# Attention and MLP mixer on one core: batches in pairs on 128 partitions, attention in 64x64 array tiles, TensorE order by hand

## The chip, the cores and the metric

One core of one Trainium2 chip. The metric is the device time of one execution in microseconds (us). The engines are TensorE (PE, with its weight loads shown apart as PEld), VectorE (DVE), ScalarE (ACT), GpSimd (POOL) and SyncE (SP, which only issues DMA here). No second core runs, so a run is called fast when it lies within 1.5% of the fastest of the same kernel. Medians are over all runs of a kernel.

## The reference, cut to what matters

```python
# attention: 8 batches, 12 heads, 448 positions, 64 wide
scores = matmul(q, k^T) / 8 - log(448)
x = matmul(1 / (1 + exp(-scores)), v)          # heads side by side: x is [8, 448, 768]

# mixer: token sizes 448 -> 256 -> 448, channel sizes 768 -> 1536 -> 768
h = relu(x^T @ w_tok1) @ w_tok2
u = x + h^T
out = u + relu(u @ w_ch1) @ w_ch2              # float32
```

## The kernel before

Both kernels load or cast to 16 bits and accumulate in 32-bit PSUM. The sequence of 448 is split as position = 4p + j with p on 112 partitions. One batch is one unit of work: its attention is woven with the mixer of the batch before it, and a scheduler decides TensorE's final order.

```python
J = 4; P = S // J                      # 112 partitions
# loads: POOL queue, 32 to 16 bit in flight, runs of 64 floats (256 bytes)
nc.gpsimd.dma_start(out=t_ap, in_=src[b].rearrange("h (p j) e -> p j h e", j=J))

# scores of ONE head: hi picks 64 of 128 rows of the array; the next matmul uses the same rows
for half, ps in ((0, ta), (1, tb)):
    for ci in range(2):
        nc.tensor.matmul(out=ps[:, ci, 0:S],
            lhsT=qkTt[64*hi : 64*hi+64, 1, 2*half+ci, :],
            rhs=qkTt[64*hi : 64*hi+64, 0, :, :], ...)
    # ... sigmoid by ACT, 112 x 896 at a time

# attention times V: the two heads of a pair fill the two column halves
for hi in (1, 0):
    for c in (3, 2, 1, 0):
        nc.tensor.matmul(out=xat[64*hi : 64*hi+64, :], lhsT=vf[:, c, h, :], rhs=at[:, c, :], ...)

# second token product, made twice: transposed (input of the channel stage) and natural
def ytrans(db, ps):   # 2 matmuls of 448 columns, then uT = xT + ps by DVE
def ynat(j, half, ps):  # 2 matmuls of 384 columns, then u_nat = x_nat + ps by DVE
# ch1: 12 x 6 matmuls of 448 columns; ch2: 8 x 12 of 384 columns, 112 rows of output each

for b in range(B):
    ac = attention_chunks(b + 1) if b + 1 < B else []
    weave(ac, mixer_chunks(b))
```

Of the kernel before, what the change touches and what calls it, by code (L numbers as in the profile page):

```python
# [19 lines left out]
def kernel(  # L20
# [10 lines left out]
):  # L31
    nc = tc.nc
# [5 lines left out]
    J = 4  # L38
    P = S // J
    NPAIR = H // 2  # L40
    NDB = D // 128
    NCB = CC // 128
    DH = D // 2
    att_scale = 1.0 / math.sqrt(E)
# [9 lines left out]
    make_identity(nc, ident)  # L54
    bias_t = pc.tile([128, 1], FP32, name="att_bias")
    nc.vector.memset(bias_t[:, :], att_bias)

    par = {"qk": 0, "m": 0}

    w_tok1_t = pc.tile([P, J, TT], FP16, name="w_tok1_t")  # L60
# [5 lines left out]
    qkv_tiles = {}  # L66
    xmem = {}

    def emit_qkv_dma(b):
        qf = pa.tile([P, J, H, E], FP16, tag="qkv", bufs=6, name=f"q_f16_{b}")  # L70
        kf = pa.tile([P, J, H, E], FP16, tag="qkv", bufs=6, name=f"k_f16_{b}")
        vf = pa.tile([P, J, H, E], FP16, tag="qkv", bufs=6, name=f"v_f16_{b}")
        for t_ap, src in ((qf, q), (kf, k), (vf, v)):
            nc.gpsimd.dma_start(  # L74
                out=t_ap[:, :, :, :],
                in_=src[b].rearrange("h (p j) e -> p j h e", j=J),
            )
        qkv_tiles[b] = (qf, kf, vf)

    def emit_weight_dma():  # L80
        nc.gpsimd.dma_start(
            out=w_tok1_t[:, :, :], in_=moe_w_tok1.rearrange("(p j) t -> p j t", j=J)
        )
        nc.gpsimd.dma_start(
            out=w_tok2_s[:, :, :], in_=moe_w_tok2.rearrange("(tc t) s -> t tc s", tc=2)
        )
        nc.gpsimd.dma_start(
            out=w_ch1_t[:, :, :], in_=moe_w_ch1.rearrange("(db d) c -> d db c", db=NDB)
        )
        nc.gpsimd.dma_start(  # L90
            out=w_ch2_t[:, :, :], in_=moe_w_ch2.rearrange("(cb c) d -> c cb d", cb=NCB)
        )
        nc.vector.tensor_copy(
            out=w_tok2_n[:, :, :, :],
            in_=w_tok2_s.rearrange("t c (p j) -> t c j p", j=J),
        )

    def attention_chunks(b):
        qf, kf, vf = qkv_tiles[b]
        qkT = {}  # L100
        attnT = {}
        xT = pa.tile([128, NPAIR, S], FP16, tag="xT", bufs=2, name=f"xT_{b}")
        x_nat = pa.tile([P, J, D], FP16, tag="x_nat", bufs=2, name=f"x_nat_{b}")
        xmem[b] = (xT, x_nat)

        def t_full(pair):
            def f():
                tqt = pp.tile([128, 2, J, P], FP16, tag="t", bufs=1, name=f"tq_{b}_{pair}")
                for qk0, src in ((1, kf), (0, qf)):
                    for j in range(J):  # L110
                        nc.tensor.transpose(  # L111
                            out=tqt[:, qk0, j, :],
                            in_=src[:, j, 2 * pair : 2 * pair + 2, :],
                            identity=ident[:P, :P],
                        )
                qkTt = pa.tile(
                    [128, 2, J, P], FP16, tag="qkT", bufs=3, name=f"qkT_{b}_{pair}"
                )
                nc.vector.tensor_copy(out=qkTt[:, :, :, :], in_=tqt[:, :, :, :])  # L119
                qkT[pair] = qkTt  # L120

            return f

        def qk_group(i, hi):
            def f():
                at = pa.tile(
                    [P, J, S], FP16, tag="attnT", bufs=3, name=f"attnT_{b}_{i}_{hi}"
                )
                attnT[(i, hi)] = at
                pq = par["qk"]  # L130
                ta = pp.tile([P, 2, 512], FP32, tag=f"qk{pq}", bufs=1, name=f"qkA_{b}_{i}_{hi}")
                tb = pp.tile([P, 2, 512], FP32, tag=f"qk{1 - pq}", bufs=1, name=f"qkB_{b}_{i}_{hi}")
                par["qk"] ^= 1
                qkTt = qkT[i]
                for half, ps in ((0, ta), (1, tb)):
                    for ci in range(2):
                        nc.tensor.matmul(  # L137
                            out=ps[:, ci, 0:S],
                            lhsT=qkTt[64 * hi : 64 * hi + 64, 1, 2 * half + ci, :],
                            rhs=qkTt[64 * hi : 64 * hi + 64, 0, :, :],  # L140
                            start=True,
                            stop=True,
                        )
                    nc.scalar.activation(  # L144
                        out=at[:, 2 * half : 2 * half + 2, :],
                        in_=ps[:, :, 0:S],
                        func=SIGMOID,
                        bias=bias_t[:P, :],
                        scale=att_scale,
                    )  # L150

            return f

        def av_chunk(pair):
            def f():
                xat = pp.tile([128, S], FP32, tag="xa", bufs=1, name=f"xa_{b}_{pair}")
                for hi in (1, 0):
                    at = attnT[(pair, hi)]
                    h = 2 * pair + hi
                    for c in (3, 2, 1, 0):  # L160
                        nc.tensor.matmul(  # L161
                            out=xat[64 * hi : 64 * hi + 64, :],
                            lhsT=vf[:, c, h, :],
                            rhs=at[:, c, :],
                            start=(c == 3),
                            stop=(c == 0),
                        )
                nc.scalar.activation(out=xT[:, pair, :], in_=xat[:, :], func=COPYF)

            return f  # L170

        def bt_double(pair):
            def f():
                xb = pp.tile(
                    [P, J, 2, 128], FP16, tag="t", bufs=1, name=f"xb_{b}_{pair}"
                )
                for pi in (1, 0):
                    for j in range(J):
                        nc.tensor.transpose(  # L179
                            out=xb[:, j, pi, :],  # L180
                            in_=xT[:, pair + pi, 112 * j : 112 * j + 112],
                            identity=ident[:, :],
                        )
                nc.vector.tensor_copy(  # L184
                    out=x_nat[:, :, 128 * pair : 128 * pair + 256], in_=xb[:, :, :, :]
                )

            return f

        chunks = [t_full(0), t_full(1)]  # L190
        for i in range(NPAIR):
            chunks.append(qk_group(i, 0))
            if i + 2 < NPAIR:
                chunks.append(t_full(i + 2))
            if i >= 1:
                chunks.append(av_chunk(i - 1))
            chunks.append(qk_group(i, 1))
            if i == 3 or i == 5:
                chunks.append(bt_double(i - 3))
        chunks.append(av_chunk(NPAIR - 1))  # L200
        chunks.append(bt_double(NPAIR - 2))
        return chunks

    def mixer_chunks(b):
        xT, x_nat = xmem[b]
        chunks = []

        h1T = pa.tile([128, 2, D], FP16, tag="h1T", bufs=2, name=f"h1T_{b}")
        uT = pa.tile([128, NDB, S], FP16, tag="uT", bufs=1, name=f"uT_{b}")
        u_nat = pa.tile([P, J, D], FP32, tag="u_nat", bufs=1, name=f"u_nat_{b}")  # L210
        h2aT = pa.tile([128, NCB, S], FP16, tag="h2aT", bufs=1, name=f"h2aT_{b}")
        outs = pa.tile([P, J, D], FP32, tag="outs", bufs=1, name=f"outs_{b}")

        def tok1(half, tcb, ps):
            for j in range(J):
                nc.tensor.matmul(  # L216
                    out=ps[:, :],
                    lhsT=w_tok1_t[:, j, 128 * tcb : 128 * tcb + 128],
                    rhs=x_nat[:, j, DH * half : DH * half + DH],
                    start=(j == 0),  # L220
                    stop=(j == J - 1),
                )
            nc.scalar.activation(
                out=h1T[:, tcb, DH * half : DH * half + DH], in_=ps[:, :], func=RELU
            )

        def ytrans(db, ps):
            for tcb in (1, 0):
                nc.tensor.matmul(
                    out=ps[:, :],  # L230
                    lhsT=h1T[:, tcb, 128 * db : 128 * db + 128],
                    rhs=w_tok2_n[:, tcb, :, :],
                    start=(tcb == 1),
                    stop=(tcb == 0),
                )
# [97 lines left out]
    for c in attention_chunks(0):  # L333
        c()
# [35 lines left out]
```

## Time and profile before

| quantity | before |
|---|---|
| median, 4 runs | 543.12 us (541.00 to 544.24) |
| span of the profiled run | 541.1 us |
| TensorE busy | 94% |
| first matmul | 15.3 us |
| attention of batch 0 without a mixer | up to about 67 us, counted back from the later batches |
| then seven woven batches | 60.18 us each |
| last mixer and store | the remaining 52.4 us |

From the page of the kernel before come three lines: busy time by engine (share of the span, number of instructions), TensorE's busy tenths in 40 equal slices, and the shares of the chain of work that ended last.

```profile
PE 508.4 (94%) x3040; PEld 284.0 (52%) x3040; DVE 201.1 (37%) x346; ACT 225.8 (42%) x273; POOL 58.7 (11%) x34
...
PE   0789899999999999999999999999999999998994
...
PE 92%; DVE 3%; DMA 2%; ACT 1%; issue 1%; POOL 0%; POOLq 0%; DVEq 0%; ACTq 0%
```

TensorE binds: the chain runs through it for 92% of the span. The next view is the busy time by engine in chosen stretches of the same kernel (stretch, its length, busy us and instructions of each engine, granted clock, DMA share, GB/s).

```profile
30.00:90.00 60.00, 56.72 (x246) 24.07 (x245) 14.86 (x26) 34.68 (x41) 9.09 (x4) 1.00 1.94 116
210.00:270.00 60.00, 59.87 (x381) 34.18 (x379) 24.93 (x43) 27.99 (x34) 6.84 (x3) 1.00 0.63 58
```

In the woven stretch the first pair of numbers says that TensorE stood still for 0.13 of 60 us. Busy is not the same as well used, though. The timeline shows it (start, length, engine, line, operation, out<-in, partitions x elements, count). Lengths overlap, because matmuls are pipelined; the useful number is the distance from one start to the next.

```profile
22.70 0.95 PE L137 MATMUL qkA_0_1_138<-qkT_0_104 64*112 64x448 f16 x2
...
199.28 0.38 PE L161 MATMUL xa_0_1631<-attnT_0_1_1578,v_f_3_927 112*64 112x448 f16 x1
199.30 0.38 PE L161 MATMUL xa_0_1631<-attnT_0_0_1550,v_f_3_927 112*64 112x448 f16 x1
199.50 0.35 PE L161 MATMUL xa_0_1631<-attnT_0_1_1578,v_f_3_927 112*64 112x448 f16 x1
199.51 0.35 PE L161 MATMUL xa_0_1631<-attnT_0_0_1550,v_f_3_927 112*64 112x448 f16 x1
...
200.17 0.58 PE L137 MATMUL qkA_1_1_1642<-qkT_1_1536 64*112 64x448 f16 x2
200.59 0.54 PE L137 MATMUL qkB_1_1_1643<-qkT_1_1536 64*112 64x448 f16 x2
201.06 0.37 PE L242 MATMUL yn1a_1650<-h1T_1499,w_tok_n 128*112 128x384 f16 x1
```

Two value matmuls (L161), one per column half, start 0.02 us apart and the next two 0.2 us later: two share the time of one. The scores (L137) use 64 of 128 rows and get no such company: four of them take 0.89 us, from 200.17 to 201.06, so 0.22 each. At 22.70 the same pair of scores is listed with 0.95 us instead of 0.58: TensorE ran at half clock during the first stage. The trace's own clock record agrees: its first entry is full clock from 72.23 us on. The window view prints a granted clock of 1.00 before that only because the record has no entry there.

### The profile page before, as it was taken

Reading aid. Unit: us, or ns where it says so; the run is one execution under the profiler, and the core shown is the slowest. Engines: PE = TensorE matmul, PEld = TensorE weight load, DVE = VectorE, ACT = ScalarE, POOL = GpSimd, SP = SyncE. Lnnn points to the kernel's source line nnn. Section 1 sums busy time; section 2 is a strip of 40 time slices with the busy share of each in tenths; the row PEclk is TensorE's granted clock in tenths of the full one; section 3 lists DMA queues with packets and bytes.
Section 4 is the critical chain, followed back from the end, with each engine's and each line's share of the span. In section 5 each row is a group of like instructions: output and inputs, shape, how many; then the busy total and the mean of one; then the engine's idle time right before and its main releaser. Section 6 shows DMA issues by size and latency. Waiting matters only on the chain.

```text
span 541.1 us, 6968 instructions
## 1 busy us (share of the span) xinstructions
PE 508.4 (94%) x3040; PEld 284.0 (52%) x3040; DVE 201.1 (37%) x346; ACT 225.8 (42%) x273; POOL 58.7 (11%) x34
## 2 busy tenths in 40 slices
PE   0789899999999999999999999999999999998994
PEld 0433354576456654565456654565456644574463
DVE  0200054424542265324542264324542363325431
ACT  0356455424734274525634274435633274331000
POOL 8303300201030001101030102001000000000000
PEclk9999999999999999999999999999999999999998
DMA  9999980906497090909195190909000200002002
GB/s 98 185 212 164 132 52 2 102 2 126 28 60 43 28 127 1 102 1 143 12 76 28 60 95 6 97 1 154 1 1 0 98 7 1 1 1 102 1 1 102
DMA packets 133198, 33.14 MB, mean 61 GB/s; under 512 B 129600, under 2 KB 131392, under 8 KB 132272
## 3 DMA queue, kind: packets, MB, share of 16 engines
q0 software_dynamic: 132144, 21.69, 62.6%
q1 hardware_dynamic: 1024, 11.01, 6.1%
q8 instruction: 23, 0.38, 0.3%
q14 instruction: 7, 0.06, 0.0%
HBM read 43.38 MB, written 11.01 MB: 101 GB/s over the span
## 4 chain that ended last, share of the span: by engine, by line
PE 92%; DVE 3%; DMA 2%; ACT 1%; issue 1%; POOL 0%; POOLq 0%; DVEq 0%; ACTq 0%
DMA k_f_0_77<-in_k_dram 2%; DVE h2aT_4318 L265 1%; PE xa_4_310 L161 0%; PE xa_0_166 L161 0%; PE xa_3_282 L161 0%; PE xa_2_244 L161 0%; PE xa_1_205 L161 0%; POOL q_f_0_76 L74 0%; DVE u_nat_4317 L249 0%; PE c_0a_4496 L271 0%; PE c_0a_4144 L271 0%; PE c_0a_3584 L271 0%; PE c_1a_3055 L271 0%; PE c_0a_3018 L271 0%; PE c_2a_2527 L271 0%
## 5 line engine op out<-in xcount | busy, mean ns | idle before, releaser
L258 PEld LDWEIGHTS <-w_ch_t 128*128 128x128 f16 x576 | 53.3, 98 | 57.5 <-issue 13.4
L242 PEld LDWEIGHTS <-w_tok_n 128*112 128x112 f16 x128 | 13.7, 128 | 14.3 <-issue 13.3
L216 PEld LDWEIGHTS <-w_tok_t 112*128 112x128 f16 x128 | 11.6, 102 | 10.1 <-issue 5.7
L111 PE MATMUL tq_0_95<-ident,k_f_0_77 112*128 112x112 f16 x4 | 0.6, 294 | 15.3 <-DMA k_f_0_77<-in_k_dram 15.3
L271 PEld LDWEIGHTS <-h2aT_4318 128*112 128x112 f16 x96 | 12.4, 130 | 4.4 <-DVE h2aT_4318 L265 1.3
L271 PEld LDWEIGHTS <-h2aT_936 128*112 128x112 f16 x96 | 12.2, 130 | 3.9 <-issue 1.0
L271 PEld LDWEIGHTS <-h2aT_2068 128*112 128x112 f16 x96 | 12.2, 130 | 3.9 <-issue 1.0
L271 PEld LDWEIGHTS <-h2aT_2634 128*112 128x112 f16 x96 | 12.2, 130 | 3.9 <-issue 1.0
L271 PEld LDWEIGHTS <-h2aT_370 128*112 128x112 f16 x96 | 12.2, 130 | 3.9 <-issue 1.0
L271 PEld LDWEIGHTS <-h2aT_1502 128*112 128x112 f16 x96 | 12.2, 130 | 3.9 <-issue 1.0
L271 PEld LDWEIGHTS <-h2aT_3760 128*112 128x112 f16 x96 | 12.2, 130 | 3.9 <-issue 1.0
L271 PEld LDWEIGHTS <-h2aT_3200 128*112 128x112 f16 x96 | 12.2, 130 | 3.9 <-issue 1.0
L111 PEld LDWEIGHTS <-k_f_0_77 112*128 112x128 f16 x24 | 2.2, 130 | 20.4 <-DMA k_f_0_77<-in_k_dram 15.3
L161 PEld LDWEIGHTS <-v_f_0_78 112*64 112x64 f16 x48 | 4.2, 150 | 9.6 <-issue 9.6
L144 ACT ACTIVATE attnT_0_0_117<-qkA_0_0_118,att_bias 112x896 f16<-112x896 f32 x1 | 1.0, 1007 | 16.6 <-PE qkA_0_0_118 L137 16.6
L119 DVE COPY qkT_0_104<-tq_0_95 128x896 f16<-128x896 f16 x1 | 0.6, 625 | 15.4 <-PE tq_0_95 L111 15.4
L74 POOL DMA_DIRECT2D v_f_7_3191<-in_v_dram x1 | 2.3, 2279 | 30.1 <-PE xa_5_3168 L161 30.1
L74 POOL DMA_DIRECT2D v_f_3_927<-in_v_dram x1 | 2.3, 2277 | 30.1 <-PE xa_5_904 L161 30.1
L74 POOL DMA_DIRECT2D v_f_4_1493<-in_v_dram x1 | 2.3, 2277 | 30.1 <-PE xa_5_1470 L161 30.1
L74 POOL DMA_DIRECT2D v_f_5_2059<-in_v_dram x1 | 2.3, 2277 | 30.1 <-PE xa_5_2036 L161 30.1
L74 POOL DMA_DIRECT2D v_f_6_2625<-in_v_dram x1 | 2.3, 2277 | 30.1 <-PE xa_5_2602 L161 30.1
L184 DVE COPY x_nat_94<-xb_4_349 112x1024 f16<-112x1024 f16 x1 | 0.7, 691 | 11.8 <-PE xb_4_349 L179 11.8
(1442 smaller groups left out, 1233.5 us busy)
## 6 DMA issues: line engine op xcount, KB each, us to landing
w_ch_t<-in_moe_w_ch_dram POOLq DMA_DIRECT2D x2, 2304.0 KB, 26.8
out_dram<-outs_371 SPq DMA_DIRECT2D x1, 1344.0 KB, 6.4
out_dram<-outs_937 SPq DMA_DIRECT2D x1, 1344.0 KB, 6.4
out_dram<-outs_1503 SPq DMA_DIRECT2D x1, 1344.0 KB, 6.3
out_dram<-outs_2069 SPq DMA_DIRECT2D x1, 1344.0 KB, 6.4
out_dram<-outs_2635 SPq DMA_DIRECT2D x1, 1344.0 KB, 6.4
out_dram<-outs_3201 SPq DMA_DIRECT2D x1, 1344.0 KB, 6.2
out_dram<-outs_3761 SPq DMA_DIRECT2D x1, 1344.0 KB, 6.2
```

The source lines that it names most:

```text
L74: nc.gpsimd.dma_start(out=t_ap[:, :, :, :], in_=src[b].rearrange("h (p j) e -> p j h e", j=J),)
L111: nc.tensor.transpose(out=tqt[:, qk0, j, :], in_=src[:, j, 2 * pair : 2 * pair + 2, :], identity=ident[:P, :P],)
L119: nc.vector.tensor_copy(out=qkTt[:, :, :, :], in_=tqt[:, :, :, :])
L144: nc.scalar.activation(out=at[:, 2 * half : 2 * half + 2, :], in_=ps[:, :, 0:S], func=SIGMOID, bias=bias_t[:P, :], scale=att_scale,)
L161: nc.tensor.matmul(out=xat[64 * hi : 64 * hi + 64, :], lhsT=vf[:, c, h, :], rhs=at[:, c, :], start=(c == 3), stop=(c == 0),)
L184: nc.vector.tensor_copy(out=x_nat[:, :, 128 * pair : 128 * pair + 256], in_=xb[:, :, :, :])
L216: nc.tensor.matmul(out=ps[:, :], lhsT=w_tok1_t[:, j, 128 * tcb : 128 * tcb + 128], rhs=x_nat[:, j, DH * half : DH * half + DH], start=(j = ...
L242: nc.tensor.matmul(out=ps[:, :], lhsT=w_tok2_n[:, tcb, j, :], rhs=h1T[:, tcb, DH * half : DH * half + DH], start=(tcb == 1), stop=(tcb == 0),)
L258: nc.tensor.matmul(out=ps[:, :], lhsT=w_ch1_t[:, db, 128 * cb : 128 * cb + 128], rhs=uT[:, db, :], start=(db == NDB - 1), stop=(db == 0),)
L265: nc.vector.tensor_scalar(out=h2aT[:, cb, :], in0=ps[:, :], scalar1=0.0, scalar2=None, op0=MAX)
L271: nc.tensor.matmul(out=ps[:, :], lhsT=h2aT[:, cb, 112 * j : 112 * j + 112], rhs=w_ch2_t[:, cb, DH * half : DH * half + DH], start=(cb == N ...
```

## The change

The intent is to fill the array. Two batches share the partitions (64 positions of each, sequence = 7p + j), so the mixer works on all 128 rows. In attention a matmul is 64x64, and four of them (two heads by two batches, each in another quarter of the array) follow each other. The channel stage gets its input by transposing the finished natural sum rather than by a second token product. Loads go in pieces of one head pair and in runs of 1792 bytes, K before Q (before, Q came first). Q and K go over SP, and POOL casts them (DVE the very first pair); V is cast in flight. TensorE's order is fixed by hand.

```diff
-    J = 4
+    J = 7
     P = S // J
+            for b in range(2):      # load: 64 partitions per batch, one head pair
+                eng.dma_start(
+                    out=t[64 * b : 64 * b + 64, :, :, :],
+                    in_=src[2 * g + b, 2 * i : 2 * i + 2].rearrange("h (p j) e -> p h j e", j=J),
+                )
 # ... cut: for Q and K eng is SP and a POOL copy casts to 16 bits; for V it is POOL, cast in flight
+        def scores(i, j):
+            for b in range(2):
+                for h in range(2):
+                    nc.tensor.matmul(
+                        out=ps[64 * b : 64 * b + 64, h, 0:S],
+                        lhsT=kT[i][64 * h : 64 * h + 64, j, b, :],
+                        rhs=qT[i][64 * h : 64 * h + 64, b, :, :], ...)
 # ... cut: one sigmoid of 128 x 896
+        def values(i):
+            for j in range(J):
+                for h in range(2):
+                    for b in range(2):
+                        nc.tensor.matmul(
+                            out=ps[b][64 * h : 64 * h + 64, :],
+                            lhsT=vf[64 * b : 64 * b + 64, h, j, :],
+                            rhs=attn[(i, j)][64 * b : 64 * b + 64, h, :], ...)
 # ... cut: copies to xT by ACT; back(i): seven transposes into the natural layout
-        def ytrans(db, ps):
+        def tok2(j):       # natural sum u by DVE, then a 16-bit copy u16 of it by DVE
+        def uturn(j):      # six transposes of u16, copied to uT by ACT
 # ... cut: ch1 in pieces of 512 and 384 columns, ch2 14 x 12 matmuls of 384 columns
+    with tc.manual_schedule(engines={mybir.EngineType.PE}):
+        for _, _, f in attention_atoms(0):
+            f()
+        for g in range(NG):
+            front, rest = mixer_atoms(g)     # front: first token product
 # ... cut: rest is woven with attention_atoms(g + 1) by weights in us
```

Below, a group is a pair of batches, and the first stage is the attention of group 0, which runs without a mixer.

## The prediction

> **What bounds it now.** TensorE. The busy table gives it 94% of 541 us, the chain of waits 92%; ACT has 42%, DVE 37%, POOL 11%. Three stages (timeline): the first matmul starts at 15.3 us, waiting for K by DMA. Batch 0's attention runs alone to about 67 us, with 448-column matmuls 0.37 us apart; from about 72 us on the pitch is 0.19. The Trainium skill, "TensorE: Matmul & The Clock Gate", Part 1, has these two states (half clock until the array is kept busy); the PEclk row does not show it. From 90 to 450 us the windows show TensorE busy 59.87 of each 60 us, 381 matmuls: 60 us per batch, 120 per pair. The last mixer takes 490 to 533, then some 7 us of eviction and store.
>
> **Warm pitches (timeline).** 448 columns 0.190, 384 columns 0.163, 128-column transpose 0.056, 64-row scores 0.21. Two 64-column value matmuls already start 0.01-0.02 us apart, 0.19 per pair: column tiles overlap. A change of tile shape costs some 0.1 us (eight value matmuls: 0.89 instead of 0.76). Before, pitches sum to about 55 of 60 us; the rest is switches and unpaired value matmuls.
>
> **After, TensorE per pair of batches** (estimate from these pitches): ch1 72x0.217+72x0.163=27.4; ch2 168x0.163=27.3 (fewer than 192, all 128 rows full instead of 112); transposes 168x0.056=9.4; tok1 and tok2 each 28 concurrent pairs, 4.6; scores and values each 42 quads of 0.19 if all four tiles overlap, 8.0; sum 89. The transposed token product (24 matmuls of 448, 4.6 us per pair of batches) goes; 42 transposes, 2.4 us, come. Shape switches about 60x0.1=6, small waits 3-5: about 99 us a pair instead of 120. The skill, "TensorEngine Tiling (Array Packing)", Key Properties, says that tiles run independently and that a mode switch drains; the trace shows the overlap for two tiles, none for four.
>
> **Other engines per pair:** ACT 42x0.91 for sigmoids (batch-0 spacing) plus 12x0.5, 8x0.45, 7x0.7: about 53; DVE about 41; POOL 12 casts and 12 V issues. None binds except locally: the token stage needs about 1.8 us of DVE per j against 1.0 of TensorE.
>
> **Stages.** Smaller, contiguous 1792-byte loads on SP: first matmul at about 8 us. Attention of pair 0 alone: ACT 44 us, TensorE at half clock about 50-56, in-order waits: ends near 70. Three woven groups of 99: 367. Last mixer without attention: 4.6+12+55=72: 439. Evictions and store now go by 128x768 pieces: +3.
>
> **Predicted: 442 us, range 416 to 472.** Nearly all of the gain lies on the critical path, since TensorE bounds. Chances: faster 0.97, within 2% 0.015, slower 0.015.
>
> **Shown right by:** four score matmuls starting within about 0.05 us, some 0.2 us per quad; windows of about 99 us per group with TensorE above 93% busy; pair 0's half-clock pitch to about 70 us; DMA packets far fewer, first matmul near 8 us.
>
> **Wrong if:** four tiles overlap only in twos (0.38 per quad: +16 us per group, about 495 in all); weight loads of 64 columns serialise the quads (0.25: +5 per group); the fixed order leaves TensorE waiting for PSUM banks, the token stage's DVE or POOL casts; w_ch2, queued on POOL behind casts, lands after 80 us and stalls; or pair 0's attention runs at full clock (-12).

## The result, and the profile after

The changed kernel took 435.87 us (median of 4, 434.59 to 439.55) against 543.12 before. The ratio is 0.8031, 95% interval 0.7986 to 0.8076. Ratios are the mean time of one kernel's fast runs over that of the other's in the same rounds, so not quite the ratio of the medians quoted. Outputs are correct.

The same three lines of the page of the changed kernel:

```profile
PE 396.2 (92%) x3712; PEld 215.7 (50%) x3712; DVE 174.8 (40%) x312; ACT 216.8 (50%) x277; POOL 74.5 (17%) x105
...
PE   1775668999999999999999999999999999999995
...
PE 85%; ACT 7%; issue 3%; DVE 2%; DMA 1%; SPq 0%; ACTq 0%; DVEq 0%
```

Its busy times in three stretches: first stage, woven, last mixer.

```profile
30.00:60.00 30.00, 17.90 (x272) 9.90 (x272) 5.34 (x9) 26.77 (x33) 11.57 (x15) 1.00 1.10 255
210.00:240.00 30.00, 30.00 (x296) 17.10 (x295) 11.56 (x22) 15.70 (x19) 6.01 (x8) 1.00 0.43 104
390.00:433.00 43.00, 38.11 (x235) 22.71 (x233) 14.46 (x26) 0.00 (x0) 0.00 (x0) 0.98 0.26 65
```

And its timeline in a woven group:

```profile
94.05 0.36 PE L147 MATMUL qk_1_2_1295<-qT_1_1207,kT_1_1206 64*64 64x448 f16 x4
94.23 0.35 PE L168 MATMUL xa_0_0_1302<-attn_0_0_1095,v_0_914 64*64 64x448 f16 x1
94.24 0.35 PE L168 MATMUL xa_0_1_1303<-attn_0_0_1095,v_0_914 64*64 64x448 f16 x1
94.24 0.35 PE L168 MATMUL xa_0_0_1302<-attn_0_0_1095,v_0_914 64*64 64x448 f16 x1
94.25 0.35 PE L168 MATMUL xa_0_1_1303<-attn_0_0_1095,v_0_914 64*64 64x448 f16 x1
94.42 0.35 PE L168 MATMUL xa_0_0_1302<-attn_0_1_1102,v_0_914 64*64 64x448 f16 x1
```

Four score matmuls (one row, x4) take 0.18 us before the values start, and four value matmuls start within 0.02 us of each other, the next four 0.19 us after the first. TensorE still binds, but in the first stage it now idles: ACT is busy 26.77 of 30 us there, TensorE 17.90.

The spans divide like this. A boundary is the first matmul of a group's first token product. In the kernel before, that of batch 0 already starts at 55.77 us, because the scheduler mixes it with the attention of batch 1; there the end of the first stage is counted back from batch 1's (127.61 us) by one repeat of 60.18.

| stage | before | after | difference |
|---|---|---|---|
| to the end of the first stage | 67.4 us, attention of 1 batch | 67.65 us, attention of 2 batches | +0.2 |
| woven | 7 x 60.18 = 421.3 us | 3 x 97.15 = 291.5 us | -129.8 |
| last mixer, eviction, store | 52.4 us, 1 mixer | 73.7 us, 2 mixers | +21.3 |
| span | 541.1 | 432.8 | -108.3 |

The first row hides a difference of the clock: from the first matmul on, the kernel before had 56.9 us at half clock, the changed one 24.4 in its first stage (clock records).

Where a woven pair of batches gained is seen by charging to each group of matmuls the time until the next group starts, so that waits and changes of tile shape are included:

| TensorE us per two batches | before | after |
|---|---|---|
| scores | 21.98 | 10.08 |
| attention times V | 11.99 | 8.58 |
| ch1 | 28.37 | 28.39 |
| ch2 | 32.22 | 28.15 |
| first token product | 6.12 | 4.66 |
| second token product, natural | 6.59 | 6.84 |
| the same transposed, or transposes of the sum | 4.99 | 2.94 |
| transposes of Q and K, and of attention | 8.11 | 7.52 |
| sum | 120.37 | 97.16 |

Half of the 23.2 us is in the scores alone.

### The profile page after: what moved, and what is told of

Same layout as the page of the kernel before. It is cut to its first block, busy times and chain, and to the rows that moved or that the text cites. A ratio compares the mean times of both kernels' runs of the same rounds, so it can differ in the third digit from the quotient of the medians.

```text
span 432.8 us, 8713 instructions
## 1 busy us (share of the span) xinstructions
PE 396.2 (92%) x3712; PEld 215.7 (50%) x3712; DVE 174.8 (40%) x312; ACT 216.8 (50%) x277; POOL 74.5 (17%) x105
## 4 chain that ended last, share of the span: by engine, by line
PE 85%; ACT 7%; issue 3%; DVE 2%; DMA 1%; SPq 0%; ACTq 0%; DVEq 0%
DMA rawq_0_76<-in_q_dram 1%; PE xa_5_0_787 L168 1%; PE xa_0_0_273 L168 1%; PE c_2_5_1_4890 L286 0%; PE c_2_4_1_4846 L286 0%; PE c_2_4_0_4809 L286 0%; PE c_2_3_1_4746 L286 0%; PE c_2_2_0_4654 L286 0%; PE c_2_1_1_4615 L286 0%; PE c_2_0_0_4490 L286 0%; PE c_1_6_0_3556 L286 0%; PE c_1_5_1_3507 L286 0%; PE c_1_4_1_3463 L286 0%; PE c_1_4_0_3426 L286 0%; PE c_1_3_1_3363 L286 0%
## 5 line engine op out<-in xcount | busy, mean ns | idle before, releaser
L286 PEld LDWEIGHTS <-h2aT_4980 128*128 128x128 f16 x168 | 16.4, 98 | 10.9
L286 PEld LDWEIGHTS <-h2aT_3597 128*128 128x128 f16 x168 | 15.6, 98 | 12.5 <-issue 3.2
L286 PEld LDWEIGHTS <-h2aT_2214 128*128 128x128 f16 x168 | 15.6, 98 | 12.5 <-issue 3.2
L286 PEld LDWEIGHTS <-h2aT_831 128*128 128x128 f16 x168 | 15.6, 98 | 12.5 <-issue 3.2
L240 PEld LDWEIGHTS <-w_tok_n 128*64 128x64 f16 x224 | 12.1, 108 | 9.0 <-issue 4.8
L222 PEld LDWEIGHTS <-w_tok_t 64*128 64x128 f16 x224 | 10.6, 94 | 7.8 <-issue 1.0
L131 PE MATMUL tk_0_165<-ident,k_0_74 128*128 128x128 f16 x7 | 0.9, 311 | 7.3 <-DVE k_0_74 L83 7.3
L154 ACT ACTIVATE attn_0_0_184<-qk_0_0_183,att_bias 128x896 f16<-128x896 f32 x1 | 1.0, 1007 | 10.1 <-PE qk_0_0_183 L147 10.1
L131 PEld LDWEIGHTS <-k_0_74 128*128 128x128 f16 x7 | 0.7, 141 | 7.3 <-DVE k_0_74 L83 7.3
L99 DVE COPY w_tok_n<-w_tok_s 128x896 f16<-128x896 f16 x1 | 1.6, 1562 | 5.5 <-DMA w_tok_s<-in_moe_w_tok_dram 5.5
L147 PEld LDWEIGHTS <-kT_0_163 64*64 64x64 f16 x28 | 1.1, 129 | 4.7 <-issue 4.5
L83 DVE CAST k_0_74<-rawk_0_71 128x896 f16<-128x896 f32 x1 | 1.1, 1086 | 5.3 <-DMA rawk_0_71<-in_k_dram 5.3
L83 POOL CAST k_5_3738<-rawk_5_3735 128x896 f16<-128x896 f32 x1 | 0.9, 933 | 12.4 <-issue 12.4
L147 PEld LDWEIGHTS <-kT_2_329 64*64 64x64 f16 x28 | 0.9, 104 | 4.3 <-issue 3.5
L83 POOL CAST k_4_3725<-rawk_4_3722 128x896 f16<-128x896 f32 x1 | 0.9, 934 | 12.4 <-issue 12.4
L83 POOL CAST k_4_959<-rawk_4_956 128x896 f16<-128x896 f32 x1 | 0.9, 933 | 12.4 <-issue 12.4
L83 POOL CAST k_4_2342<-rawk_4_2339 128x896 f16<-128x896 f32 x1 | 0.9, 933 | 12.4 <-issue 12.4
L147 PEld LDWEIGHTS <-kT_5_669 64*64 64x64 f16 x28 | 0.9, 106 | 4.3 <-issue 3.3
L75 POOL DMA_DIRECT2D v_3_953<-in_v_dram x2 | 1.2, 593 | 10.2 <-DMA w_ch_t<-in_moe_w_ch_dram 10.2
```

The lines of the kernel that those rows point to most:

```text
L75: eng.dma_start(out=t[64 * b : 64 * b + 64, :, :, :], in_=src[2 * g + b, 2 * i : 2 * i + 2].rearrange("h (p j) e -> p h j e", j=J),)
L83: eng.tensor_copy(out=t[:, :, :, :], in_=raw.rearrange("p h j e -> p j h e"))
L99: nc.vector.tensor_copy(out=w_tok2_n[:, :, :, :], in_=w_tok2_s.rearrange("t c (p j) -> t c j p", j=J),)
L131: nc.tensor.transpose(out=ps[:, j, :, :], in_=src[:, j, :, :], identity=ident[:, :])
L147: nc.tensor.matmul(out=ps[64 * b : 64 * b + 64, h, 0:S], lhsT=kT[i][64 * h : 64 * h + 64, j, b, :], rhs=qT[i][64 * h : 64 * h + 64, b, :, ...
L154: nc.scalar.activation(out=at[:, :, :], in_=ps[:, :, 0:S], func=SIGMOID, bias=bias_t[:, :], scale=att_scale,)
```

## The experiments

All the runs below gave correct results. "Changed" is the kernel after; its median is 435.87, and 439.69 when run again. "Changed, again" shares its rounds with the last three runs of the table only; the others are compared with the changed kernel through their ratios to the kernel before, and by their traces.

| run | median us | ratio to before (95%) | first stage ends at us | woven group us |
|---|---|---|---|---|
| changed | 435.87 | 0.8031 (0.7986 to 0.8076) | 67.65 | 97.15 |
| changed, again | 439.69 | 0.8072 (0.8036 to 0.8108) | 74.32 | 97.15 |
| values one tile at a time | 481.28 | 0.8864 (0.8817 to 0.8912) | 84.62 | 107.65, the first 109.24 |
| values in row pairs | 451.09 | 0.8307 (0.8282 to 0.8331) | 73.94 | 100.52 |
| scheduler's order | 432.37 | 0.7942 (0.7904 to 0.7980) | 59.42 | 98.18, the first 101.42 |
| token product twice | 445.62 | 0.8201 (0.8177 to 0.8226) | 68.01 | 98.47 |
| cast in DMA | 438.46 | 0.8040 (0.8005 to 0.8075) | 70.50 | 97.15, the first 98.23 |
| before, score row pairs | 504.85 | 0.9256 (0.9208 to 0.9305) | | 2 x 56.60 |
| first copies on DVE | 444.41 | 0.8144 (0.8083 to 0.8205) | 73.43 | 97.15 |
| first stage reordered | 429.60 | 0.7874 (0.7831 to 0.7917) | 59.65 | 97.15, the first 97.82 |
| its order alone | 432.93 | 0.7942 (0.7910 to 0.7975) | 66.44 | 97.15, the first 97.50 |
| attention in token stage | 437.75 | 0.8001 (0.7955 to 0.8046) | 72.86 (slow profile) | 96.72 |
| first stage and token | 428.40 | 0.7869 (0.7836 to 0.7901) | | 96.72 |

### Values one tile at a time

```diff
-            for j in range(J):
-                for h in range(2):
-                    for b in range(2):
+            for h in range(2):
+                for b in range(2):
+                    for j in range(J):
                         nc.tensor.matmul(out=ps[b][64*h : 64*h+64, :], ...)
```

> The changed kernel with the value product in another order: all seven matmuls of one 64x64 tile in a row, then the next tile. Same matmuls, same banks. Theory A (the gain needs neighbours on different tiles): a value product of 28 matmuls grows from about 1.4 us (quads of 0.19) to about 5.3 to 5.9 us, some 25 us more per woven group, and the attention alone at the start also grows; in all 520 to 545 us. Theory B (tiles overlap whatever the order, or the gain comes from elsewhere): within 1% of the changed kernel, 431 to 440.

Measured 481.28 us, 10.5 us more per woven group. The order matters, so theory B falls; but the loss is under half of what theory A said. One value product takes 3.21 us rather than 5.3. The starts of its matmuls, read from the trace in one woven group (us after 220; program order is tile 1 complete, tile 2 complete, and so on; each row is one tile, assigned by its 0.19 us rhythm):

```
tile 1:  0.441 0.630 0.819 1.008 1.198 1.387 1.576
tile 2:                    1.014 1.228 1.417 1.606 1.795 1.984 2.173
tile 3:  1.612 1.825 2.014 2.203 2.393 2.582 2.771
tile 4:                    2.209 2.423 2.612 2.801 2.990 3.179 3.368
```

Tile 2 starts just when the fourth matmul of tile 1 has started and three are left. So tiles do run independently, and part of the overlap is recovered even in a bad order, as if TensorE looked three matmuls ahead; that reading is inferred from these starts, not tested by itself. A record doesn't name its tile, so the assignment is inferred too. It is supported by the semaphore signals, which sit on the last matmul of tile 3 (2.771) and of tile 4 (3.368): tile 4 began before tile 3 had ended.

### Values in row pairs

```diff
-            for j in range(J):
-                for h in range(2):
+            for h in range(2):
+                for j in range(J):
                     for b in range(2):
```

> As the run before, but the value product goes in pairs that share the column half and differ in the row half. Theory A (row halves overlap as column halves do): pairs of 0.19, a value product of 2.7 us, 8 us more per group, in all 460 to 472. Rival (only column halves overlap): as slow as one tile at a time, 520 to 545.

Measured 451.09 us, woven groups 100.52, a value product 2.02 us. Row halves overlap as column halves do, so the rival falls. Theory A's number was again too high (at 0.19 per pair, 14 pairs would have taken 2.7 us); the same look-ahead would explain it.

### TensorE's order left to the scheduler

```diff
-    with tc.manual_schedule(engines={mybir.EngineType.PE}):
+    with ExitStack():
```

> The changed kernel with TensorE's order left to the scheduler, as in the kernel before; nothing else. The list shows that most quads stay together, while in the first stage value matmuls and scores are mixed. Theory A (tiling and full partitions carry the gain, the fixed order hardly any): 430 to 445. Rival (the fixed order is a main part): above 450.

Measured 432.37 us: theory A's range. The fixed order is no part of the gain: the two intervals, from different sessions, even lie just apart in the scheduler's favour. The order is worth about 1 us in a woven group (97.15 against 98.18), and more in the first one (101.42), but the scheduler's first stage ended at 59.42 us instead of 67.65. The timeline of the scheduler's version in its first woven group:

```profile
68.47 0.37 PE L147 MATMUL qk<-qT,kT 64*64 64x448 f16 x1
68.78 0.52 PE L240 MATMUL yn<-h1T,w_tok_n 128*64 128x384 f16 x4
69.22 0.56 PE L147 MATMUL qk<-qT,kT 64*64 64x448 f16 x5
```

A quad of scores is torn into one and three (the three run on into two of the next quad, hence x5), and each piece pays a slot and a change of tile shape: the scores of a woven group cost 12.26 us here and 10.08 in the fixed order. In the first stage the scheduler put scores between value matmuls, and only 11.8 us of that stage were at half clock, against 25.3 in the changed kernel (classed by length, see below). How much of the shorter stage is the order and how much the clock, this run doesn't separate.

### The token product twice

```diff
-        def uturn(j): ...                       # 42 transposes of u16 per group, copies by ACT
+        def ytrans(db):                         # 24 matmuls of 448 columns per group
+            # out=ps[b], lhsT=h1T[:, b, tcb, 128*db : 128*db+128], rhs=w_tok2_n[:, tcb, :, :]
+            # uT = xT + ps by DVE
-            u16 = ...                           # the 16-bit copy of u
```

> The changed kernel with the channel input made as before: the token product a second time in transposed form, plus the transposed attention, by VectorE; no 16-bit copy of the sum, no transposes of it. Theory A: TensorE 2 us more per group (24 matmuls of 0.19 for 42 transposes of 0.07), and VectorE about 3 us more in the token stage, which it paces: 442 to 456 in all. Rival (the transposed sum costs more than it saves, by its wait for the copy): 428 to 436.

Measured 445.62 us, in theory A's range; woven groups 98.47. In the ledger the transposed product costs 5.49 us where the transposes cost 2.94, and the natural one falls from 6.84 to 5.97, for a reason not tested. The spans of two profiles at like clock (0.994 both) agree piece by piece: 0.4 us in the first stage, 3 x 1.32 in woven groups, 2.7 in the last mixer, together the 7.0 us between 439.8 and 432.8. So transposing the sum is part of the gain: those 7 us are 1.6% of the span.

### Q and K cast in DMA

```diff
-        eng = nc.gpsimd if what == "v" else nc.sync
+            order = "h (p j) e -> p j h e"        # runs of 256 bytes, 16-bit on arrival
+            nc.gpsimd.dma_start(...)              # no SP load, no POOL copy
```

> The changed kernel with Q and K loaded as before: by the POOL queue, cast to 16 bits in flight, in runs of 256 bytes, with no POOL cast. Theory A (the new loads matter at the start only): first matmul at 9 to 11 us instead of 7.3, weights of the channel stage land later and the first channel product waits; 440 to 465 in all, woven groups two and three unchanged at about 97. Rival (loads are off the critical path): 434 to 440.

Measured 438.46 us, between the two runs of the changed kernel: the rival. The first matmul is at 7.2 us all the same, so neither the long runs nor the SP queue is needed to move it from 15.3 to 7.3; what is left of the change is the smaller first piece, and K before Q (in the kernel before, Q landed at 10.47 us and K, which the first matmul needs, at 15.24). The GB/s of the view (135 from 10 to 30 us, 255 in the changed kernel) can't be compared as they stand, since a load that is cast in flight counts with its 16-bit bytes; by the 32-bit bytes read, they are 269 and 326. The Trainium skill, "DMA: Bandwidth & Descriptors", Specifications, asks for 512 bytes or more per transfer for line rate; the trace agrees: a packet of 128 bytes (a run of 256 after the cast) took 32 ns, one of 1792 bytes 109 ns, four times as many bytes per ns. In the whole time no cost can be told from the noise (intervals 0.8005 to 0.8075 and 0.8036 to 0.8108 for the changed kernel again); only the first woven group is 1.1 us longer.

### The kernel before, with row pairs of scores

```diff
-        def qk_group(i, hi):       # one head, four pieces of 112 keys
+        def qk_group(i, half):     # both heads, two pieces of 112 keys
-                for half, ps in ((0, ta), (1, tb)):
-                    for ci in range(2):
+                for ci, ps in ((0, ta), (1, tb)):
+                    for hi in range(2):
                         nc.tensor.matmul(
-                            out=ps[:, ci, 0:S],
+                            out=ps[:, hi, 0:S],
                             lhsT=qkTt[64 * hi : 64 * hi + 64, 1, 2 * half + ci, :], ...)
 # ... cut: value matmuls alternate hi; attention tiles reshaped to match, four buffers
```

> The kernel before, with one thing alone: the scores of the two heads of a pair, which lie in the two row halves, follow each other (and value matmuls alternate as far as the scheduler lets them). Batches are not paired, nothing else changes. Theory A (most of the gain in attention needs row neighbours, not the pairing of batches): scores 0.19 to 0.22 per pair instead of 0.43, some 5 us less per batch; 480 to 505 in all. Rival (the gain needs 64x64 tiles and the pairing): 533 to 543.

Measured 504.85 us: theory A, at the upper end of its range. The timeline of a woven batch of this kernel:

```profile
200.13 0.40 PE L137 MATMUL qkA<-qkT 64*112 64x448 f16 x2
200.36 0.35 PE L137 MATMUL qkB<-qkT 64*112 64x448 f16 x2
200.91 0.35 PE L258 MATMUL c_10a<-uT,w_ch_t 128*128 128x448 f16 x1 [0.20 <-DVE h2aT L265]
```

Two scores now take 0.23 us where two took 0.42. The order of scores and values (with four attention buffers instead of three) brings 40.6 us (545.47 to 504.85), over a third of the whole gain, without pairing a batch. In the profiled spans, 21.5 us come from six repeats that are 3.59 us shorter each: per two batches the scores fall from 21.9 to 15.7 us and the values from 12.0 to 10.8. The time up to the first ch2 gives 16.0 us; half clock also fell there, from 56.9 us to 32.9 us by the clock records, so how much of the 16.0 is overlap alone isn't shown.

### First copies on DVE

```diff
-                nc.scalar.activation(out=xt[:, :, b, :], in_=..., func=COPYF)
+                if g == 0: nc.vector.tensor_copy(out=xt[:, :, b, :], in_=...)
+                else:      nc.scalar.activation(...)
```

> The changed kernel, with the copies of the attention output in pair 0 (the stage without a mixer) moved from ACT to DVE. Theory A (this stage is bound by ACT: 44.6 of 59.6 us busy, and 1 us waits where TensorE transposes first): 12 x 0.45 = 5 us less, the token product starts at 61 to 64 instead of 67.7, in all 429 to 432. Rival (bound by TensorE in half clock, or by loads): no change, 434 to 438.

Measured 444.41 us, which no theory named; the first stage ended at 73.43 us. Taking 5 us of work from ACT won nothing; that it lost is not shown, since the changed kernel itself ended this stage at 67.65 and 74.32 us, and the interval overlaps that of the changed kernel again. The timeline of the changed kernel, with the waits in brackets, tells why nothing was won, and the last row is the same step of this run, two head pairs earlier (both at full clock):

```profile
49.97 0.54 ACT L178 ACTIVATE xT_3_629<-xa_3_1_600 128x448 f16<-128x448 f32 x1
50.57 0.56 PE L187 MATMUL xb_3_632<-ident,xT_3_629 128*128 128x128 f16 x7 [1.07 <-ACT xT_3_629 L178]
51.06 0.38 PE L147 MATMUL qk_4_2_641<-qT_4_552,kT_4_551 64*64 64x448 f16 x4
51.56 1.01 ACT L154 ACTIVATE attn_4_2_642<-qk_4_2_641,att_bias 128x896 f16<-128x896 f32 x1 [1.05 <-PE qk_4_2_641 L147]
```

```profile
37.08 3.70 ACT L154 ACTIVATE attn<-qk,att_bias 128x896 f16<-128x896 f32 x4 [2.21 <-PE qk L147]
```

The fixed order makes a loop: TensorE waits for the copies (1.07 us) to transpose them back, only then issues the next scores, and ACT waits for those (1.05 us). Moving the copies off ACT leaves the loop as long; ACT just waits 2.21 us instead of copying for 0.9 and waiting for 1.05.

The move also had a price of its own, once. On DVE these copies stood behind one that waited for a token weight to land:

```profile
24.76 1.54 DVE L99 COPY w_tok_n<-w_tok_s 128x896 f16<-128x896 f16 x1 [5.79 <-DMA w_tok_s<-in_moe_w_tok_dram]
26.23 1.14 DVE L180 CAST xT<-xa 128x448 f16<-128x448 f32 x2
```

TensorE waited 3.51 us for them, and ACT's next sigmoid started at 28.93 us instead of 26.55 in the changed kernel.

### First stage reordered

```diff
+        if g == 0:
+            for s in range(NP * J):                       # scores one by one
+                atoms.append((s / 2, 0.22, lambda s=s: scores(s // J, s % J)))
+                # values of pair i in two parts, with a score between them;
+                # back(i) only after two more scores
```

(and the copies on DVE, as in the run before)

> The run before, with TensorE's order in pair 0 changed too: scores one by one, the value product in two parts between them, the transposes back after the next scores, so that ACT always has scores waiting. Theory A (ACT binds): 42 sigmoids at 0.90 from 12.3 us on end near 51, token product at 55 to 59, in all 422 to 428. Rival (loads or TensorE bind by then): 428 to 434.

Measured 429.60 us, in the rival's range, near its edge to theory A's. The first stage ended at 59.65 us, where theory A hoped for 55 to 59. Stretches of the changed kernel and of this one, both at full clock (the fourth pair of numbers is ACT):

```profile
30.00:40.00 10.00, 5.85 (x85) 3.08 (x85) 1.78 (x3) 8.95 (x11) 3.77 (x4) 1.00 1.09 247
```

```profile
30.00:40.00 10.00, 7.40 (x121) 4.58 (x121) 3.90 (x7) 9.66 (x12) 3.08 (x4) 1.00 1.08 247
```

ACT is at 9.66 of 10 us, and no longer spends any of them on copies: in this stretch ACT binds. Before it, from 20 to 30 us, it was busy for only 5.5 of 10: half clock, and again the copies behind the token weight on DVE (an ACT wait of 3.58 us).

### The changed kernel again, and the order alone

> The changed kernel itself, unaltered, on the chip of the three runs that follow, to compare with. 434 to 440, woven groups of 97.15, token product of pair 0 at about 67.6.

Measured 439.69 us (436.21 to 441.92). The woven groups repeat to 0.01 us, but the first stage ended at 74.32 us, not 67.65: that is the whole difference of the two spans (439.5 and 432.8). The same transposes in the two runs, the first kernel run, then the second:

```profile
37.30 0.55 PE L131 MATMUL tq_3_458<-ident,q_3_127 128*128 128x128 f16 x7
```

```profile
37.52 0.95 PE L131 MATMUL tq<-ident,q 128*128 128x128 f16 x7
```

And the second run's busy times and granted clock from 30 to 50 us:

```profile
30.00:50.00 20.00, 14.53 (x153) 7.99 (x150) 3.74 (x6) 14.25 (x18) 6.47 (x8) 0.66 1.10 250
```

The second ran at half clock for most of that stretch, and its granted clock there is 0.66. Classing every matmul of the first stage by its length gives 25.3 us at half clock in the first run and 50.4 us in the second (by the clock records, 24.4 and 48.9). The token-twice kernel has the same first stage but for more buffers: 26.1 us, end at 68.01. The run with more attention in the token stage, below, has the same first stage too: 42.6 us by the clock record, end at 72.86. So one program has a first stage of 67 to 74 us, longer with more time in half clock. This set a noise of some 6 us under the runs that change only this stage.

The order alone, with ACT copying again:

```diff
-                if g == 0:
+                if g < 0:      # copies on ACT in every group
```

> The order of the first stage of e9 alone, with the attention copies back on ACT. Moving the copies alone made the first stage longer (73.4), order and copies together shorter (59.7). Theory A (the fixed order makes a loop in which ACT waits for TensorE, which waits for ACT's copy; order breaks it, and then ACT binds): first stage 62 to 66, in all 430 to 435. Rival (only both together help, since ACT binds in any case): 66 or more, 435 to 440.

(e9 is the run "first stage reordered".) Measured 432.93 us against 439.69 in the same rounds, intervals apart (0.7910 to 0.7975 and 0.8036 to 0.8108). The time is in theory A's range; the first stage (66.44) is in the rival's, by 0.44 us. Half clock differs between these profiles (classed by length, 36.4 us here and 19.3 with order and copies together), so the stage ends alone can't settle it. Counting the sigmoids that start between the first and the last of the stage, by the clock record, can:

| first stage | sigmoids at full clock | at half clock |
|---|---|---|
| changed | 28 in 34.1 us, 0.82 per us | 13 in 17.2 us, 0.75 |
| changed, again | 13 in 17.1 us, 0.76 | 28 in 40.1 us, 0.70 |
| copies alone | 22 in 30.7 us, 0.72 | 19 in 26.2 us, 0.72 |
| order alone | 24 in 23.9 us, 1.00 | 17 in 24.8 us, 0.69 |
| both | 32 in 30.8 us, 1.04 | 9 in 13.3 us, 0.68 |

At full clock the order alone speeds the stage up and the copies alone don't (their 0.72 includes the wait behind the token weight): breaking the loop is what mattered. Once it is broken the copies add little. At half clock none of these is faster than the changed kernel.

### More attention in the token stage

```diff
-            rest.append((0.65, lambda j=j: tok2(j)))
+            rest.append((1.1, lambda j=j: tok2(j)))
-                rest.append((0.35, lambda j=j: uturn(j - 2)))
+                rest.append((0.6, lambda j=j: uturn(j - 2)))
```

> The changed kernel with one thing alone: the weights by which attention is woven into the token stage raised from 0.65 and 0.35 to 1.1 and 0.6, so that more of the next pair's attention stands there, where DVE paces TensorE (1.40 us per step against 1.25). Theory A (TensorE waits in the token stage, and attention fills it): woven groups 95 to 96.5 instead of 97.15, in all 430 to 435. Rival (the token stage of woven groups is already full): 97.0 to 97.5, no change.

In the changed kernel's last mixer, the timeline of DVE shows the pace of the token stage:

```profile
367.95 0.55 DVE L247 TENSOR_TENSOR u_2_5083<-x_nat_3748,yn_2_1_5090 128x384 f32<-128x384 f16 x1
368.41 0.55 DVE L247 TENSOR_TENSOR u_3_5106<-x_nat_3748,yn_3_0_5107 128x384 f32<-128x384 f16 x1
368.88 0.55 DVE L252 CAST u_3_2_5096<-u_2_5083 128x768 f16<-128x768 f32 x1
369.35 0.55 DVE L247 TENSOR_TENSOR u_3_5106<-x_nat_3748,yn_3_1_5113 128x384 f32<-128x384 f16 x1
```

Three operations 0.47 us apart, without a pause: 1.40 us per step. Measured 437.75 us, not told apart from 439.69 (intervals 0.7955 to 0.8046 and 0.8036 to 0.8108). Groups took 96.72 us in its profile; the profile of the next run has the same 96.72. So 0.43 us per group, between the two ranges. Attention in this place fills little.

### First stage and token stage together

```diff
+        first.append((14.3, 1.15, mixer0[0][0][1]))   # token product of heads 0 to 5
+        first.append((17.3, 1.15, mixer0[0][1][1]))   # inside the first stage, ReLU on DVE
 # ... plus the reordered first stage and the weights of the run before
```

> The best version so far (copies of pair 0 on DVE, its order changed) with the weights of the run before, and with the first half of pair 0's token product inside the attention stage (its ReLU on DVE). Theory: 2.3 us less TensorE after the first stage, woven groups as in the run before; 420 to 427. Rival (the early product disturbs the stage it is put into, or the weights give nothing): 427 to 431, as e9.

Measured 428.40 us, inside the rival's range. In the profiles the early token product won nothing: the rest of that product began at 64.6 us and group 1 at 160.0, where the reordered kernel without it had started the whole product at 59.65 and group 1 at 157.5. But half clock up to the end of the first stage was 25.8 us here and 18.6 there (clock records), so what the early product is worth by itself isn't shown. Still, it is 2.5% faster than the changed kernel in the same rounds (0.7869 / 0.8072 = 0.975, computed from the two ratios), and the fastest kernel, with the reordered one beside it.

## Why the prediction was right

The time was predicted as 442 us, 416 to 472; measured 435.87. In its own terms: 70 + 3 x 99 + 72 + 3 became 67.65 + 3 x 97.15 + 69.0 + 4.7.

- **TensorE binds, and the gain is in woven groups.** Right. The estimate of 89 us of pitches plus switches and waits was 99; the ledger has 97.16. Term by term, the ledger (which includes switches and waits) lies above the pitches, by little except for scores and tok2: ch1 27.4 and 28.39, ch2 27.3 and 28.15, transposes 9.4 and 10.46, scores and values 8.0 each and 10.08 and 8.58, tok2 4.6 and 6.84. The excess over the pitches is 8 us, where 9 to 11 was allowed.
- **Four tiles overlap.** Right, and shown by the two orders that take it away (one tile 10.5 us more per group, row pairs 3.4). The skill's "TensorEngine Tiling (Array Packing)", Key Properties, says that tiles work independently; the traces agree, with four starts within 0.02 us.
- **What carries the gain.** The prediction credited the whole change. The scores alone give 11.9 of 23.2 us per pair of batches. In the old kernel, row neighbours (of scores above all, 6.2 us per two woven batches) give 40.6 us in total without any pairing. Full partitions are seen in ch2 (4.1 us in the ledger; no run isolates them), not in ch1, whose streamed columns are the same 896 per pair of batches. The fixed order is not a gain in total.
- **The first stage.** Predicted to end near 70 with half clock up to then, and 12 us earlier at full clock. It ended at 67.65, but half clock took only 25 us of it: that the number fits is luck. The in-order waits, which the prediction named without a size, were the loop between TensorE and ACT, and they made up for the half clock that did not come. With the loop broken, the stage ended at 66.44 with 36.4 us at half clock, and at 59.65 with 19.3 (changed: 67.65 with 25.3, 74.32 with 50.4).
- **Loads.** First matmul at 8 us: right (7.3). The reason given, contiguous loads on SP, was not: 256-byte runs start as early. The size of the first piece, and K before Q, are what is left, and the runs did not test them.
- **Token stage.** Predicted as 1.8 us of DVE per step against 1.0 of TensorE. Measured 1.40 of DVE. That DVE paces it was right, where it was read, in the last mixer.
- **Pairing has a price that the prediction counted.** The stages at both ends, which have no partner to overlap with, now hold two batches: +21 us at the end, and hardly any change at the start.

What stays open: why the clock drops in the first stage in one run and not in the next. No run forced it. That the stage is longer with more half clock is what four profiles of it (one slow) agree on (24.4, 25.2, 42.6 and 48.9 us at half clock; ends at 67.65, 68.01, 72.86 and 74.32), not an intervention.

## What to carry to other kernels

Before changing a layout, look whether small matmuls that stand next to each other use different halves of the array: here matmul order, with one more buffer, brought over a third of the gain. A fixed engine order needs a look at every loop through another engine, above all in stages where nothing else is woven in. Before moving work to an idle engine, look at what stands ahead of it in that engine's order. And when two batches become one unit, count the unwoven stages at both ends, which grow with the unit.

## What the Trainium skill lacked or had wrong

- "TensorE: Matmul & The Clock Gate", Part 3, "What overlaps and what doesn't", says that matmuls start and end in strict program order. Across tiles the trace speaks against it for starts, if its records are assigned to tiles by their 0.19 us rhythm as above: with one tile at a time, the second tile's first matmul started at 221.014 us, before the fifth to seventh of the first tile (221.198 to 221.576). A look-ahead of three matmuls fits the 3.21 us of that product; no page has it.
- "TensorEngine Tiling (Array Packing)", Key Properties, says that a mode change drains the array, but gives no cost. From 64x64 scores to a full-array matmul the last slot was 0.29 us (99.16 to 99.45) instead of 0.18 to a value quad (94.05 to 94.23): about 0.1 us per change.
- "TensorE: Matmul & The Clock Gate", Part 1, calls the warm-up penalty under 1% of a typical kernel's span. That is said of the first warm-up alone. Here the clock fell again later in the stage, and two profiled runs of one program differed by 6.7 of 433 us (1.5%), all of it in the first stage, with 25.3 and 50.4 us at half clock.
- No page says that a trace's clock record can begin with the first change: in the changed kernel its first entry is full clock at 28.36 us, and the view prints 1.00 before that for want of an entry, while seven transposes are listed at 0.93 us, which take 0.55 later. Lengths of matmuls show the clock there.
